# A block sum of a Winograd second layer, made by accumulating DMAs in place or by VectorE into a block of its own

## The chip, the cores and the metric

The kernel runs on one core of one Trainium2 chip. The metric is the device time of one execution in microseconds (us). TensorE (PE in the profile) does the matrix products, VectorE (DVE) and ScalarE (ACT) the elementwise work and the copies out of PSUM; GpSimd (POOL) here mostly issues DMAs, and SyncE (SP) issues the others. DMAs issued by POOL appear in the profile as queue q0 ("software_dynamic"), those of SP and ACT as q1 ("hardware_dynamic"); both are carried by the same 16 DMA engines.

## The reference

An attention with eight heads (three plain causal, five with a sink of 4 and a window of 64), whose output of 3072 tokens by 512 channels is the input of a mixture of four experts. Every token goes through all four:

```python
def _moe_ref(x, domain_probs, w1, w2):
    p = domain_probs / (domain_probs.sum(-1, keepdims=True) + 1e-09)
    out = np.zeros((N, D), dtype=np.float32)          # N 3072, D 512
    for e in range(E):                                # E 4
        h = np.maximum(x @ w1[e], 0.0)                # 512 -> 1024
        out += p[:, e:e + 1] * (h @ w2[e])            # 1024 -> 512
    return out.astype(np.float32)
```

## The kernel before

The tokens are cut into 24 tiles of 128. Tiles 0 to 3 go through both layers directly. The other 20 go two at a time, in ten **pairs** that are called here by their first tile: 4, 6, 8, ... 22. `pair_steps` makes one pair. Its inputs are scaled by the probabilities first (`scale_inputs`), so the second layer of all four experts is one product: hidden values of a pair (256 tokens, 4 x 1024 deep) by `w2` (4 x 1024 by 512).

That product is done with seven block products in place of eight (Strassen's scheme in Winograd's form). The hidden values lie in one SBUF tile `hA` (fp16) of five blocks, each 128 partitions by 16 x 128 elements. Four are the 2 x 2 blocks of the hidden values: A11 and A21 for the first half of each expert's hidden units (first and second token tile), A12 and A22 for the other half. Of the 16 columns of a block (`k`), four belong to each expert: 0 to 3 to expert 0, 4 to 7 to expert 1 and so on. The operand sums are

- S1 = A21 + A22 (`first_sum`),
- S2 = S1 - A11 (`second_sum`, in place of A11),
- S3 = A22 - S2 (`third_sum`),
- S4 = A12 - S2 (`fourth_sum`, in place of A12).

Before the change S1 has the fifth block and S3 takes the place of A21.

The order on TensorE within a pair: first layer 1, expert by expert; then the seven products, each of 16 matmuls with 256 columns (line 1387), in the order A11, A12, S2, S1, S3, S4, A22. Between their halves, steps of the attention of later tokens are put in until about pair 16. `second_sum(0)` makes the columns of experts 0 and 1 after the first product, `second_sum(1)` those of experts 2 and 3 in the middle of the second product. The third product is the first that reads S2.

Layer 1 has two forms. `plain_layer1(e)` yields four steps of eight matmuls (line 1207), each followed by a ReLU on ScalarE (line 1216) that writes two blocks for two columns. `winograd_layer1(e)` yields seven steps of eight small matmuls (line 1236); the last block that it writes is A21, by a ReLU on ScalarE at its end (line 1286). Which expert takes which form depends on the pair:

- pairs 4 to 16: experts 0, 1, 2 plain (twelve steps in that order), expert 3 by Winograd, mixed in;
- pair 18: experts 0 and 1 plain, 3 and 2 by Winograd;
- pair 20: experts 3 and 2 by Winograd, then expert 1 by Winograd mixed with expert 0 plain;
- pair 22, the last: all four by Winograd.

The order of the instructions on each engine is the order in which the program emits them (a manual schedule); `order` in `pair_steps` is a list of steps with an operation to emit after each group of steps. Every engine takes its own instructions strictly in turn. Waits are put in by dependency: an instruction waits until the last writer or reader of what it touches is done. A wait of a DMA is taken by the engine that issues it, before it issues.

POOL's queue also holds the loads of the attention, in the program's order: for each step of the attention five loads of values into `vS` (line 306), each waiting for the matmuls that read the old values, then three loads of keys (`k_rows`) and three of queries (`q`, line 219) and three of `vR` (line 304).

Touched by the change: the names S1, S2, S3 (line 979), `first_sum` (line 1180), and the lists in `pair_steps`.

Of the kernel before, what the change touches and what calls it, by code (L numbers as in the profile page):

```python
# [14 lines left out]
ALU = mybir.AluOpType  # L15
# [4 lines left out]
def kernel(  # L20
# [77 lines left out]
    gp = nc.gpsimd  # L98
# [9 lines left out]
    HT = F // P // 2  # L108
# [5 lines left out]
    EW = (E - 1, E - 2)  # L114
# [291 lines left out]
    for h in range(H):  # L406
        if h == 2:
            nc.sync.dma_start(
                out=v_s32, in_=v[0, :, 0:NS, :].rearrange("h r d -> r h d")
# [16 lines left out]
        out=probs,  # L426
        in_=moe_domain_probs[0 : NPL * P, :].rearrange("(t p) e -> p t e", p=P),
    )
    nc.sync.dma_start(
        out=p_in.rearrange("t x e -> t (x e)"),  # L430
        in_=moe_domain_probs.rearrange("(t x) e -> t (x e)", x=P),
# [543 lines left out]

    hA16 = hA
    blocks = hA.rearrange("p (b k x) -> p b k x", b=5, k=KT)
    A11, A21, A12, A22, S1 = (blocks[:, n, :, :] for n in range(5))
    S2, S3, S4 = A11, A21, A12

    def whole_b(k, n, e, ft):
        return w2sb[:, e * FTP + k * HT + ft, n * HN : (n + 1) * HN]
# [25 lines left out]
    def first_weight_sums(e):  # L1008

        return [  # L1010
            lambda: minus(t1[e, 0], w1_part(e, 0, 1), w1_part(e, 0, 0)),
            lambda: minus(t1[e, 1], w1_part(e, 1, 1), t1[e, 0]),
            lambda: minus(t1[e, 2], w1_part(e, 1, 0), t1[e, 1]),
            lambda: minus(w1_part(e, 0, 1), w1_part(e, 1, 1), w1_part(e, 0, 1)),
        ]
# [11 lines left out]
    EW3 = E - 3  # L1027
# [22 lines left out]
    def last_weight_sum(e):  # L1050

        minus(b_rows(0, 1, e), b_rows(1, 1, e), b_rows(0, 1, e))
# [79 lines left out]
    def load_probs(nt0):  # L1132
        pB_of[nt0] = moe.tile([P, PT, E, P], FP32, name="pB", tag="pB", bufs=1)
        rows = p_rows[nt0 : nt0 + PT, :]
        nc.sync.dma_start(
            out=pB_of[nt0].rearrange("p t e x -> p (t e x)"),
            in_=bass.AP(rows.tensor, rows.offset, [[0, P], [1, PT * E * P]]),
        )
# [8 lines left out]
    def scale_inputs(nt0, e):  # L1147

        if xs_of[0] is None:
            xs_of[0] = moe.tile([P, XS], FP16, name="xs", tag="xs", bufs=1)  # L1150
        xs = scaled(e)
        for g, c0, t0, n in pieces(nt0):
            require(g)
            xin = xT[g][:, :, c0 : c0 + n * P].rearrange("p c (t x) -> p c t x", t=n)
            o = xs[:, :, t0 * P : (t0 + n) * P].rearrange("p c (t x) -> p c t x", t=n)
            pb = pB_of[nt0][:, t0 : t0 + n, e, :]
            pb = pb.rearrange("p t (c x) -> p c t x", c=1)
            nc.vector.tensor_tensor(  # L1158
                out=o, in0=xin, in1=pb.to_broadcast([P, DMP, n, P]), op=ALU.mult
            )  # L1160
# [11 lines left out]
    def scaled_sums(e):  # L1172

        nc.vector.tensor_tensor(
            out=x_sum(e, 0), in0=x_part(e, 1, 0), in1=x_part(e, 1, 1), op=ALU.add
        )
        minus(x_sum(e, 1), x_sum(e, 0), x_part(e, 0, 0))
        minus(x_part(e, 1, 0), x_part(e, 0, 0), x_part(e, 1, 0))

    def first_sum(e, n=1):  # L1180
        k = slice(e * HT, (e + n) * HT)
        nc.vector.tensor_tensor(
            out=S1[:, k, :], in0=A21[:, k, :], in1=A22[:, k, :], op=ALU.add
        )
# [8 lines left out]
    def two(nt0):  # L1193
        return nt0 >= pairs[-LAST]

    def three(nt0):
        return nt0 >= pairs[-2]

    def pair_steps(nt0, nxt):

        def plain_layer1(e):
            xs = scaled(e)
            for f0 in range(0, FTP, 2):
                ps = bank()
                for f in range(2):
                    for ct in range(DMP):
                        nc.tensor.matmul(  # L1207
                            out=ps[:, f * PC : (f + 1) * PC],
                            lhsT=w1_tile(e, ct, f0 + f),
                            rhs=xs[:, ct, :],  # L1210
                            start=(ct == 0),
                            stop=(ct == DMP - 1),
                        )
                b0 = 2 * (f0 // HT)
                k0 = e * HT + f0 % HT
                nc.scalar.activation(  # L1216
                    out=blocks[:, b0 : b0 + 2, k0 : k0 + 2, :].rearrange(
                        "p t f x -> p f t x"
                    ),
                    in_=ps.rearrange("p (f t x) -> p f t x", f=2, t=2),  # L1220
                    func=AF.Relu,
                )
                yield 2 * DMP * mm_ns(PC), 0.5
# [69 lines left out]
        a, b = (winograd_layer1(e, *y) for e, y in zip(EW, (banks, banks[::-1])))  # L1293
        if three(nt0):
# [5 lines left out]
            b = winograd_layer1(EW[1], *more_banks, more_kept)  # L1300
            third = winograd_layer1(EW3, *banks)
            if nxt is None:
                second_set.add(0)
                fourth = winograd_layer1(0, *more_banks, more_kept)

        more, last_more = [], None
        if nt0 == pairs[-LAST - 2]:
            room_for_more_sums()
            more = first_weight_sums(EW[1])
        elif nt0 == pairs[-LAST - 1]:  # L1310
            last_more = first_weight_sums(EW[1])[3]
        elif nt0 == pairs[-3]:
            room_for_third()
            more = first_weight_sums(EW3)
            last_more = more[3]
        elif nt0 == pairs[-2]:
            room_for_fourth()
            more = first_weight_sums(0)
            last_more = more[3]
        if not two(nt0):  # L1320
            n = itertools.chain(*(plain_layer1(e) for e in range(E - 1)))
            order = (
                ((n,), lambda: scale_inputs(nt0, 1)),
                ((n,), more[0] if more else None),
                ((n, a), lambda: last_weight_sum(E - 1) if nt0 == pair0 else None),
                ((n, a), None),
                ((n, a), lambda: scale_inputs(nt0, 2)),
                ((n, a), lambda: load_probs(nxt)),
                ((n, a), more[1] if more else None),
                ((n, a), more[2] if more else None),  # L1330
                ((n, a), lambda: first_sum(0, 2)),
                ((n,), None),
                ((n, n), lambda: first_sum(2, 2)),
                ((), lambda: scale_inputs(nxt, 1) if two(nxt) else None),
            )
        elif nxt is None:
            order = (
                ((), lambda: scaled_sums(EW[1])),
                ((a, b, a, b), None),
                ((a, b, a, b), lambda: scaled_sums(EW3)),  # L1340
                ((a, b, a, b, a, b), lambda: scaled_sums(0)),
                ((third, fourth, third, fourth), lambda: first_sum(EW[0])),
                ((third, fourth, third, fourth), lambda: first_sum(EW[1])),
                ((third, fourth, third, fourth), None),
                ((third, fourth), lambda: (first_sum(EW3), first_sum(0))),
            )
        elif three(nt0):
            n = plain_layer1(0)
            order = (
                ((), lambda: scaled_sums(EW[1])),  # L1350
                ((a, b, a, b), lambda: load_probs(nxt)),
                ((a, b, a, b), None),
                ((a, b, a, b), None),
                ((a, b), lambda: scaled_sums(EW3)),
                ((n,), more[0]),
                ((third, third, n), lambda: first_sum(EW[0])),
                ((third, third, n), more[1]),
                ((third, third, n), lambda: (first_sum(EW[1]), first_sum(0))),
                ((third,), lambda: (first_sum(EW3), more[2]())),
            )  # L1360
        else:
            n = itertools.chain(plain_layer1(0), plain_layer1(1))
            order = (
                ((a, a, n), more[0] if more else None),
                ((a, a, n), lambda: load_probs(nxt) if nxt else None),
                ((a, a, n), more[1] if more else None),
                ((n,), lambda: scaled_sums(EW[1])),
                ((a, b, n), more[2] if more else None),
                ((b, b, n), lambda: first_sum(0)),
                ((b, b, n), lambda: first_sum(EW[0])),  # L1370
                ((b, n, b), lambda: (first_sum(1), first_sum(EW[1]))),
            )
        for steps, op in order:
            for x in steps:
# [98 lines left out]
        if last:  # L1473

            r = slice((nt0 + 1) * P, (nt0 + 2) * P)
            for c in (slice(0, HN // 2), slice(HN // 2, HN)):
                z = bank()[:, c]
                for k in range(KT):
                    nc.tensor.matmul(  # L1479
                        out=z,  # L1480
# [6 lines left out]
                    out=o[:, 1, c], in0=z, in1=s[:, 3, c], op=ALU.add  # L1487
# [158 lines left out]
```

## Time and profile before

| | |
|---|---|
| median of 3 runs | 376.64 us (376.29 to 377.06) |
| span of the profiled execution | 374.9 us |
| granted TensorE clock | 1.000 |
| PE busy | 367.2 us (98%) |
| VectorE busy | 284.3 us (76%), 610 instructions |
| ScalarE busy | 227.2 us (61%) |
| POOL busy | 113.1 us (30%), 155 instructions |
| q0, packets' time as a share of 16 engines' span | 58.8% |

The profiled execution's span runs from its first to its last instruction; its own time beside the unprofiled runs isn't given, and the median of those is 1.7 us above the span. The pairs take the span from about 88 us to its end. Their third products start at 107.59 (pair 4), 139.19, 168.18, 197.48, 226.98 (pair 12), 255.60, 286.88, 312.69, 337.79 (pair 20) and 363.12 us (pair 22), as the timeline of TensorE has them. In the rows of a timeline the first column is the start in us from the span's start, the second the duration in us; "x3" means that three instructions in a row are merged, and the brackets at the end say how long the engine had been idle and for what.

### The profile page before, as it was taken

The page shows a single profiled execution, that of the slowest core. Times are in us where ns is not written, and L with a number is a line of the kernel's source. Part 1 is how long each engine was busy: PE and PEld are TensorE (multiplying, and loading weights), DVE is VectorE, ACT ScalarE, POOL GpSimd, SP SyncE. Part 2 cuts the span into 40 slices and gives each one's busy share as a digit, 9 for nine tenths or more (in the row PEclk, how much of TensorE's full clock was granted, in tenths as well). Part 3 has the DMA queues.
Part 4 walks back from the last instruction along what each step waited for, and adds up shares of the span by engine and source line. Part 5 has one row for each costly group of instructions (what it writes and reads, how often), then busy time and mean ns, then how long its engine had stood idle before and what let it go on. Part 6 is the DMA issues. An engine that isn't in the chain of part 4 may idle for free.

```text
span 374.9 us, 10290 instructions
## 1 busy us (share of the span) xinstructions
PE 367.2 (98%) x4200; PEld 310.5 (83%) x4200; DVE 284.3 (76%) x610; ACT 227.2 (61%) x475; POOL 113.1 (30%) x155
## 2 busy tenths in 40 slices
PE   8899999999999999999999999999999999999996
PEld 4755466668998988999989898998899998998996
DVE  7775768697788669868658858957767868989882
ACT  3863478547785785765676955784777361450630
POOL 8924573872057038115601650320000000000000
PEclk9999999999999999999999999999999999999999
DMA  8999999999599599988904990951220300300101
GB/s 163 158 202 208 197 183 192 183 201 110 97 111 155 94 97 116 159 111 61 208 10 61 170 158 15 125 134 14 71 69 3 104 13 0 115 2 3 57 2 58
DMA packets 123748, 39.25 MB, mean 105 GB/s; under 512 B 113728, under 2 KB 116356, under 8 KB 123700
## 3 DMA queue, kind: packets, MB, share of 16 engines
q0 software_dynamic: 85824, 19.01, 58.8%
q1 hardware_dynamic: 36276, 19.18, 21.9%
q8 instruction: 33, 0.54, 0.6%
q10 hardware_dynamic: 1600, 0.39, 0.5%
q14 instruction: 15, 0.12, 0.1%
HBM read 44.89 MB, written 6.34 MB: 137 GB/s over the span
## 4 chain that ended last, share of the span: by engine, by line
PE 87%; DMA 7%; POOL 3%; DVE 1%; ACT 0%; issue 0%; POOLq 0%
PE pO L1387 31%; PE pA L1207 22%; PE pO L1236 9%; DMA w2sb<-in_moe_w_dram 7%; PE pO L1094 6%; PE pA L678 5%; PE pA L1073 5%; PE pV L1236 2%; PE pV L734 2%; PE pA L1236 2%; PE pV L806 2%; POOL vS L310 1%; POOL vR L304 1%; DVE xs L1158 1%; PE pA L1479 0%; POOL early L472 0%
## 5 line engine op out<-in xcount | busy, mean ns | idle before, releaser
L1387 PEld LDWEIGHTS <-hA 128*128 128x128 f16 x1104 | 104.9, 98 | 12.2
L1207 PE MATMUL pA<-xs,w1sb 128*128 128x256 f16 x768 | 97.2, 272 | 0.0
L1207 PEld LDWEIGHTS <-w1sb 128*128 128x128 f16 x768 | 71.8, 98 | 7.6
L1387 PE MATMUL pO<-w2sb,hA 128*128 128x256 f16 x640 | 76.7, 272 | 0.0
L696 ACT ACTIVATE es<-pA 128x384 f16<-128x384 f32 (+2 forms) x122 | 59.2, 512 | 27.1 <-PE pA L678 23.3
L1216 ACT ACTIVATE hA<-pA 128x512 f16<-128x512 f32 x96 | 57.2, 597 | 29.0 <-PE pA L1207 26.7
L306 POOL DMA_DIRECT2D vS<-in_v_dram x30 | 29.6, 986 | 111.9 <-PE pV L806 110.6
L1387 PE MATMUL pO<-tsb,hA 128*128 128x256 f16 x464 | 56.7, 272 | 0.0
L1158 DVE TENSOR_TENSOR xs<-xT,pB 128x1024 f16<-128x1024 f16 (+1 forms) x49 | 47.0, 978 | 1.4 <-DMA xT<-x_pair 1.4
L992 DVE TENSOR_TENSOR hA<-hA 128x1024 f16<-128x1024 f16 x60 | 39.5, 685 | 0.4
L1086 ACT ACTIVATE hA<-pA 128x384 f16<-128x384 f32 (+1 forms) x64 | 22.2, 385 | 19.4 <-PE pA L1073 18.7
L1236 PEld LDWEIGHTS <-w1sb 128*128 128x128 f16 x512 | 31.4, 98 | 1.4 <-issue 0.5
L1073 PE MATMUL pA<-xT,w1sb 128*128 128x384 f16 (+1 forms) x256 | 31.1, 273 | 0.7 <-DVE xT L829 0.3
L1094 PE MATMUL pO<-w2sb,hA 128*128 128x512 f16 x128 | 30.7, 379 | 0.3 <-DMA w2sb<-in_moe_w_dram 0.3
L1407 ACT COPY s<-pO 128x256 f32<-128x256 f32 x31 | 11.5, 372 | 27.7 <-PE pO L1387 21.9
L829 DVE TENSOR_TENSOR xT<-pV,rc 64x384 f16<-64x384 f32 x37 | 20.5, 555 | 10.3 <-ACT rc L834 7.9
L1073 PEld LDWEIGHTS <-w1sb 128*128 128x128 f16 x256 | 19.4, 98 | 9.7 <-issue 1.5
L824 ACT ACTIVATE rc<-pV,eps 64x384 f32<-64x384 f32 x37 | 21.3, 575 | 6.5 <-PE pV L806 5.9
L700 DVE TENSOR_TENSOR es<-es,mS 128x384 f16<-128x384 f16 (+1 forms) x40 | 13.7, 344 | 15.0 <-ACT es L696 15.0
L1246 ACT COPY s<-pO 128x512 f32<-128x512 f32 x39 | 22.7, 587 | 3.2 <-PE pO L1236 3.0
L1253 DVE CUSTOM_DVE_ANT_0 hA<-pO,s 128x512 f16<-128x512 f32 x26 | 17.7, 688 | 7.7 <-PE pO L1236 6.3
L678 PE MATMUL pA<-qT,kR 128*128 128x384 f16 (+2 forms) x120 | 22.9, 278 | 0.7 <-DVE kR L595 0.6
(170 smaller groups left out, 528.0 us busy)
## 6 DMA issues: line engine op xcount, KB each, us to landing
pB<-p_rows SPq DMA_DIRECT2D x10, 512.0 KB
out_dram<-o SPq DMA_DIRECT2D x19, 256.0 KB
w1sb<-in_moe_w_dram POOLq DMA_DIRECT2D x8, 512.0 KB, 9.2
w2sb<-in_moe_w_dram POOLq DMA_DIRECT2D x4, 1024.0 KB, 12.3
vS<-in_v_dram POOLq DMA_DIRECT2D x30, 112.0 KB, 4.3
k_rows<-in_k_dram POOLq DMA_DIRECT2D x18, 128.0 KB, 5.2
q<-in_q_dram POOLq DMA_DIRECT2D x18, 128.0 KB, 6.4
vR<-in_v_dram POOLq DMA_DIRECT2D x24, 48.0 KB, 5.8
```

The lines of the kernel that those rows point to most:

```text
L306: gp.dma_start(out=t[:, :, own_v(h)], in_=windows_of(v, b, h, c))
L678: nc.tensor.matmul(out=ps[:, o : o + nq], lhsT=key_tile(b, c, h, t), rhs=qTs[b, c][:, hp, q0 : q0 + nq], start=(n == 0 or not first), stop ...
L696: nc.scalar.activation(out=es[:, 0:cols], in_=ps[:, 0:cols], func=AF.Exp, scale=SC)
L992: nc.vector.tensor_tensor(out=out, in0=a, in1=b, op=ALU.subtract)
L1073: nc.tensor.matmul(out=pss[ft][:, 0:cols_n], lhsT=w1_tile(e, ct, ft), rhs=x[:, ct, :], start=(n == 0), stop=(n == DMP - 1),)
L1094: nc.tensor.matmul(out=ps_o, lhsT=hs[:, ft, j * P : (j + 1) * P], rhs=w2sb[:, e * FTP + ft, :], start=(ft == 0), stop=(ft == FTP - 1),)
L1158: nc.vector.tensor_tensor(out=o, in0=xin, in1=pb.to_broadcast([P, DMP, n, P]), op=ALU.mult)
L1207: nc.tensor.matmul(out=ps[:, f * PC : (f + 1) * PC], lhsT=w1_tile(e, ct, f0 + f), rhs=xs[:, ct, :], start=(ct == 0), stop=(ct == DMP - 1),)
L1216: nc.scalar.activation(out=blocks[:, b0 : b0 + 2, k0 : k0 + 2, :].rearrange("p t f x -> p f t x"), in_=ps.rearrange("p (f t x) -> p f t x" ...
L1236: nc.tensor.matmul(out=ps[:, f * P : (f + 1) * P], lhsT=w_tile(e, w[:, ct, :], f), rhs=a[:, ct, :], start=(first and f == 0 and ct == 0), ...
L1246: nc.scalar.copy(out=kept[n], in_=ps)
L1387: nc.tensor.matmul(out=ps, lhsT=a[:, k, :], rhs=b(k), start=(first and k == 0), stop=(k == KT - 1), skip_group_check=not first,)
```

## The change

`first_sum` becomes a DMA on POOL's queue that adds A22 onto A21 where A21 lies, so S1 takes the place of A21, and S3 gets the fifth block. VectorE's form remains under the name `last_first_sum`, now also in place, for the experts that a pair's layer 1 ends with. Pairs 4 to 16 each have one DMA for experts 0 and 1 (256 KB: 128 rows of 2 KB) and one for expert 3 (128 KB: 128 rows of 1 KB), with expert 2 left to VectorE; pair 18 has DMAs for experts 0 and 3, with 1 and 2 in one VectorE instruction; pair 20 DMAs for 3, 2 and 0, with 1 on VectorE; pair 22 DMAs for 3 and 2, with 0 and 1 in one VectorE instruction. In all 21 DMAs; VectorE's instructions of this kind go from 26 (14 of 128x1024, 12 of 128x512) to 10 (2 of 128x1024, 8 of 128x512).

```diff
-    A11, A21, A12, A22, S1 = (blocks[:, n, :, :] for n in range(5))
-    S2, S3, S4 = A11, A21, A12
+    A11, A21, A12, A22, S3 = (blocks[:, n, :, :] for n in range(5))
+    S1, S2, S4 = A21, A11, A12
...
     def first_sum(e, n=1):
+
+        k = slice(e * HT, (e + n) * HT)
+        gp.dma_start(out=S1[:, k, :], in_=A22[:, k, :], accum_op=ALU.add)
+
+    def last_first_sum(e, n=1):
         k = slice(e * HT, (e + n) * HT)
         nc.vector.tensor_tensor(
             out=S1[:, k, :], in0=A21[:, k, :], in1=A22[:, k, :], op=ALU.add
...
                 ((n, a), lambda: first_sum(0, 2)),
-                ((n,), None),
-                ((n, n), lambda: first_sum(2, 2)),
+                ((n,), lambda: first_sum(EW[0])),
+                ((n, n), lambda: last_first_sum(EW[1])),
...
                 ((third, fourth, third, fourth), lambda: first_sum(EW[0])),
                 ((third, fourth, third, fourth), lambda: first_sum(EW[1])),
                 ((third, fourth, third, fourth), None),
-                ((third, fourth), lambda: (first_sum(EW3), first_sum(0))),
+                ((third, fourth), lambda: last_first_sum(0, 2)),
...
                 ((third, third, n), lambda: first_sum(EW[0])),
                 ((third, third, n), more[1]),
                 ((third, third, n), lambda: (first_sum(EW[1]), first_sum(0))),
-                ((third,), lambda: (first_sum(EW3), more[2]())),
+                ((third,), lambda: (last_first_sum(EW3), more[2]())),
...
                 ((b, b, n), lambda: first_sum(0)),
                 ((b, b, n), lambda: first_sum(EW[0])),
-                ((b, n, b), lambda: (first_sum(1), first_sum(EW[1]))),
+                ((b, n, b), lambda: last_first_sum(1, 2)),
```

The four lists are those of pairs 4 to 16, of pair 22, of pair 20 and of pair 18. `EW[0]` is expert 3, `EW[1]` expert 2, `EW3` expert 1.

On POOL's queue the two DMAs of a pair stand, in pairs 4 to 12, behind the `vR` loads of the attention step before and ahead of the next `vS` loads; those of pair 14 stand behind the third of the last five `vS` loads and ahead of the other two; those of pairs 16 to 22 have nothing behind them. The orders on TensorE, ScalarE and SP stay as they were.

## The prediction, made before the changed kernel ran

> **What bounds it now.** First the chain of work that ended last (page), then the busy time of each engine over pairs 4 to 20. Columns of the second row: stretch, its length, then busy us (instructions) of PE, PEld, DVE, ACT, POOL, then clock, DMA share and GB/s.
>
> ```profile
> PE 87%; DMA 7%; POOL 3%; DVE 1%; ACT 0%; issue 0%; POOLq 0%
> 88.00:347.00 259.00, 258.87 (x3152) 235.57 (x3150) 200.10 (x425) 165.07 (x324) 54.81 (x61) 1.00 0.69 84
> ```
>
> TensorE sets the end, and from 88 to 347 us it is idle for 0.13 us in all. VectorE is busy for 200.10 of 259. So relief of VectorE can return next to nothing there, and anything that makes a third product wait is paid in full. Third, the removed work itself:
>
> ```profile
> L1182 DVE TENSOR_TENSOR hA<-hA x26: 415/677/693, 101.1 to 360.5; 128x1024 f16<-128x1024 f16 x14, 128x512 f16<-128x512 f16 x12
> who waited for it (us, times):
> ```
>
> Nothing is listed as having waited for it.
>
> **What it removes.** Twelve sums of 128x1024 by 0.685 us and four of 128x512 by 0.415 us: 8.2 + 1.7 = 9.9 us of VectorE. TensorE hides all of it, so I put the gain at 0.1 us, bounds 0 and 0.4 (the 0.13 us above, and some 0.3 us of like waits in pair 22's layer 1). S1 in A21's place costs nothing: the next pair's layer 1 overwrites A21 after the seventh product, and S1 was last read in the fourth. S3 in the fifth block costs nothing: its reader in the pair before is done more than 15 us earlier.
>
> **What it adds: a delay between the ReLU and S1.** VectorE started a sum 0.03 us after a ReLU (104.00 to 104.03). A DMA first has to be issued, moved and reported. The trace has no adding DMA. Nearest is a `vS` load that met an idle queue at 251.70, 112 KB; its window gives (packets, MB, share of 16 engines over 3.4 us; then KB and us to landing):
>
> ```profile
> q0 software_dynamic: 912, 0.11, 52.8%
> vS<-in_v_dram POOLq DMA_DIRECT2D x1, 112.0 KB, 3.4
> ```
>
> Of its 3.4 us, 0.98 is POOL's own and 1.8 packet time on each engine (52.8% of 3.4), whose packets overlap a little and lie within 1.4 us. A 128 KB sum has few long rows: 8 rows of 1 KB an engine, about 0.4 us (the output stores of 346 to 350 us: 288 packets, 34.8% of 16 x 4 us, 77 ns for 2 KB). **Low end**: 3.4 - 0.35 (POOL at 0.63, as for the `w1sb` loads) - 1.4 + 0.4, about 2.0 us. **High end**: the adding cuts rows into 128-byte pieces at the `vS` packets' 32 ns and reads twice: 128 pieces an engine, 4.1 us in place of 1.8: 5.7 us. I take 3.0 us, nearer the load, its nearest row, with a little off for long rows. For 256 KB add 0.4 to 4.1 us; I take 0.5.
>
> The Trainium skill ("Collectives: The Full Stack", The bandwidth ceiling: the fold count and why AG ≠ RS ≠ AR) speaks against the change: a DMA that adds reads two sources on one ring, and ran at half the rate of a copy. Its "DMA: Bandwidth & Descriptors" (Anatomy of one DMA — SWDGE (gpsimd) path) gives 2.0 us plus bytes at 436 GB/s, so an estimate by both pages is 2.6 us for 128 KB, against 3.4 us measured here for 112 KB in small rows; the sum below would fall by 0.4 us with it. No adding DMA is in this trace to decide it.
>
> **When it is due.** S2's first half must be written when the third product starts. The subtraction takes 0.69 us (128x1024, line 992) and I allow 0.1 us for two wake-ups, so S1 of experts 0 and 1 is due 0.79 us before the third product, that of experts 2 and 3 0.79 us before its middle. From the end of the ReLUs (lines 1216, 1286) this leaves 6.4 to 8.8 us for the first DMA and 5.5 to 7.6 us for the second in pairs 4 to 10, 14, 16; the tightest is pair 14 (248.35 to 254.81, 250.15 to 255.69). `second_sum` ran in these pairs 4.7 us or more after the ReLU, so with 3.0 to 3.5 us even VectorE's queue doesn't notice. Pair 18 leaves 9 us; pair 22 has its DMAs done 4 us ahead. Cost 0; the cover is gone above some 5 us.
>
> **Pair 20** is different: the DMA of expert 0 follows the last ReLU of plain layer 1, which is nearly the end of layer 1.
>
> ```profile
> 334.05 0.60 ACT L1216 ACTIVATE hA<-pA 128x512 f16<-128x512 f32 x1 [1.17 <-PE pA L1207]
> 334.29 3.66 PE L1387 MATMUL pO<-w2sb,hA 128*128 128x256 f16 x32
> 336.11 1.29 DVE L992 TENSOR_TENSOR hA<-hA 128x1024 f16<-128x1024 f16 x2
> 337.79 2.46 PE L1387 MATMUL pO<-tsb,hA 128*128 128x256 f16 x21
> ```
>
> The ReLU ends at 334.65, the third product starts at 337.79: S1 is due at 337.00. POOL wakes some 0.05 us after the ReLU (0.30 us after a matmul's modelled end, 103.54 to 103.84, against ScalarE's 0.25, 336.04 to 336.29). 334.70 + 3.0 = 337.70: **0.7 us** late, bounds 0 (2.0 us) and 3.4 (5.7 us). Behind the waiting `second_sum` on VectorE stand the other `second_sum` and the output sum of line 1410, whose PSUM bank the fourth product needs 1.75 us later: no further cost. Nothing else is on TensorE there to fill the gap.
>
> **Pair 12** meets loads in its queue. POOL is still issuing the `vR` loads when expert 1's ReLU ends (219.36), and q0 is full:
>
> ```profile
> 218.61 2.33 POOL L304 DMA_DIRECT2D vR<-in_v_dram  x3
> 218.76 0.60 ACT L1216 ACTIVATE hA<-pA 128x512 f16<-128x512 f32 x1 [0.72 <-PE pA L1207]
> 224.38 1.29 DVE L992 TENSOR_TENSOR hA<-hA 128x1024 f16<-128x1024 f16 x2
> ...
> vR<-in_v_dram POOLq DMA_DIRECT2D x1, 48.0 KB, 5.6
> ...
> 225.00:225.50 0.50, 0.50 (x7) 0.44 (x6) 0.50 (x2) 0.31 (x1) 0.00 (x0) 1.00 0.44 53
> 225.50:226.00 0.50, 0.50 (x7) 0.41 (x5) 0.17 (x1) 0.02 (x1) 0.00 (x0) 1.00 0.00 0
> ...
> 226.98 1.04 PE L1387 MATMUL pO<-tsb,hA 128*128 128x256 f16 x8
> ```
>
> The DMA can be issued at 220.94, but the last `vR` load, issued at 220.14, lands 5.6 us later at 225.76, its packets ending near 225.4 (DMA share 0.44, then 0.00). If the queue is served in order, the 256 KB follow: 0.65 us at 77 ns for 2 KB, 1.3 if read twice, 8.2 in doubled 128-byte pieces; I take 1.1. Plus 0.35 us to report: 226.85, due at 226.19: **0.65 us** late, bounds 0.2 and 7.8. Here `second_sum` holds VectorE 2.5 us past its old time, and masks (line 700), key copies (line 290) and later operand sums stand behind it; VectorE had 0.94 us of idle time to catch up and TensorE is 0.65 late itself, so some of it reaches a later product: **0.2 us**, bounds 0 and 1.
>
> **Moved past on the queues.** POOL's `vS` loads come more than 2 us after each pair's DMAs, except in pair 14, where the fourth (245.82) now stands behind DMAs that wait until 250.15, 5 us later; it is used by the last attention step near its end, and the fifth (251.70) moves by under 1 us: 0. SP has no new instruction; its transposes share the DMA engines with 384 KB more a pair, off the path.
>
> **Sum**: 0.7 + 0.65 + 0.2 - 0.1 = 1.45 us. The profiled span of 374.9 becomes 376.4; the runs' median stands 1.7 us above the span, so 376.64 becomes **378.1 us**.
>
> **Rivals.**
> *All hidden*: a small sum costs 2.2 us and its data run at the stores' rate. Pair 20 is then on time, pair 12 0.2 us late: 376.64 + 0.2 = 376.8 us. For it: long rows, SBUF to SBUF. Against: pair 20's 2.3 us, which the nearest row misses by 1.1.
> *The addition is slow* and most pairs pay: with 128-byte pieces read once (2.05 us of packets for 128 KB, 4.1 for 256 KB), the first DMA lands after 5.7 us, the second after 7.8, one alone after 3.65. Pair 14 is then 0.5 late, pair 12 4.5 (3.7 by its first DMA), pair 20 1.35, and VectorE's queue waits in every pair, some 1 us in all: 376.64 + 7.35 = 384.0 us. For it: no adding DMA was measured. Against: rows of 2 KB have no reason to be cut.
> *VectorE's relief shows* (faster): 9.9 us fewer on its queue bring masks and copies forward, and PE's short waits go, 0.13 us in the pairs to 20 and 0.3 in pair 22's layer 1: 376.2 us. It decides only if both late DMAs land within 2.3 us and behind no load. Against: to gain over 0.75 us there is no idle time to take.
> *It doesn't do what it says* is out: the DMAs stand on POOL's queue in program order.
>
> **How the numbers follow.** Forecast (two pairs late, own range 377.3 to 380) 0.53; all hidden 0.32; slow addition 0.11; relief 0.04, most of it for more than the rows let me see. 0.2%, 0.75 us, is about what a measurement of this kernel can tell from no change. A little of the forecast and of the relief lies within that, the slow case all beyond: faster 0.03, same 0.34, slower 0.63. The range goes from the relief's 376.2 to 381.6, where pair 12's first DMA pays 3.7 and pair 20 1.35 for once-read pieces, less 0.1; beyond lies most of the slow case.
>
> **What would show it.** Gaps of TensorE before the third product in pairs 12 and 20 alone; DMAs to `hA` landing after about 3 us, after 5 to 6 in pair 12; VectorE idle before line 992 (now 997) for a DMA there. Wrong, if these gaps are missing, if other pairs show them, or if PE's matmuls themselves slow down under the added traffic.

## The result, and the profile after

The changed kernel took a median of 379.69 us (four runs, 379.15 to 380.40) against 376.85 us of the kernel before (four runs, 376.29 to 377.65): a ratio of 1.0079, 95% interval 1.0066 to 1.0091, or 2.84 us more. The profiled execution's span is 378.1 us against 374.9.

The page of the changed kernel first: the busy time of each engine, and the chain of work that ended last, by engine.

```profile
PE 368.3 (97%) x4200; PEld 311.3 (82%) x4200; DVE 275.4 (73%) x594; ACT 227.2 (60%) x475; POOL 130.9 (35%) x176
...
PE 65%; issue 15%; DMA 10%; POOL 7%; DVE 2%; ACT 1%; POOLq 0%; SPq 0%; DVEq 0%
```

VectorE is busy for 8.9 us less (284.3 before; the prediction counted 9.9 taken off). TensorE has fallen from 87% of the chain to 65%. The chain in order of time (start, length, what) shows what has come in:

```profile
221.28 6.81 DMA hA<-hA
...
331.22 1.17 POOL hA L1183
...
337.30 2.63 DMA hA<-hA
```

It ends with two waits for adding DMAs and is followed back from each along POOL's queue, so long stretches of POOL's issuing and of its waiting ("issue") count as chain that are none: a share of the chain is not a loss. What TensorE waits for tells where the time went. The waits of TensorE come first, then one row of VectorE's; each row gives who waited, for whom, and us in total, times, the longest.

```profile
PE pO L1392 <- DVE hA L992: 1.9, 2, 1.4
...
PE pV L734 <- DVE es L700: 0.4, 1, 0.4
```

```profile
DVE hA L992 <- DMA hA<-hA: 5.1, 2, 3.6
```

Line 1392 holds the matmuls of the seven products (1387 before). Twice they waited for `second_sum` (line 992), and twice `second_sum` waited for an adding DMA. The timeline of the changed kernel puts the first of these in pair 12 (start, duration, engine, line; in brackets the idle time before and its releaser):

```profile
219.01 2.30 POOL L304 DMA_DIRECT2D vR<-in_v_dram  x3
221.28 0.96 POOL L1183 DMA_DIRECT2D hA<-hA  x1
223.66 0.86 POOL L1183 DMA_DIRECT2D hA<-hA  x1 [1.42 <-DMA v_sinks<-vS]
...
228.18 1.38 DVE L992 TENSOR_TENSOR hA<-hA 128x1024 f16<-128x1024 f16 x2 [3.57 <-DMA hA<-hA]
...
228.93 1.05 PE L1392 MATMUL pO<-tsb,hA 128*128 128x256 f16 x8 [1.37 <-DVE hA L992]
...
235.15 0.23 PE L734 MATMUL pV<-vR,es 128*128 128x65 f16 x2 [0.39 <-DVE es L700]
```

and the second in pair 20:

```profile
336.41 0.60 ACT L1221 ACTIVATE hA<-pA 128x512 f16<-128x512 f32 x1 [1.17 <-PE pA L1212]
...
337.30 0.84 POOL L1183 DMA_DIRECT2D hA<-hA  x1 [4.91 <-ACT hA L1221]
...
340.05 1.29 DVE L992 TENSOR_TENSOR hA<-hA 128x1024 f16<-128x1024 f16 x2 [1.50 <-DMA hA<-hA]
...
340.80 0.94 PE L1392 MATMUL pO<-tsb,hA 128*128 128x256 f16 x7 [0.49 <-DVE hA L992]
```

The idle time in a bracket is less than the delay, since the records of the matmuls overlap. The delay itself is read by setting the same matmul of both traces side by side. Each column gives by how much a version's matmul starts later than before's beyond what had already gathered; the first column is the lag at the third product of pair 4, the others are the steps up to the third product named, and the last goes on to the last matmul.

| | up to pair 4 | to 10 | to 12 | to 14 | to 18 | to 20 | to the end | from pair 10 on |
|---|---|---|---|---|---|---|---|---|
| after | +0.42 | 0.00 | **+1.53** | **+0.58** | -0.16 | **+0.65** | +0.18 | +2.78 |

The first 0.42 us arise around the first loads (by 20 us of the span; the first adding DMA is issued at 99.60), and up to pair 4 every profiled execution differs, from -0.24 to +1.18 in the runs below. They are no part of the change. From pair 10 on the sum is 2.78 us, against 2.84 by the medians. The 1.53 are pair 12's third product, the 0.58 an attention matmul that stands among its later products (line 734, at 235.15), the 0.65 pair 20's third product. In pairs 4 to 10, 14 and 16 nothing moved. The 0.18 arise in pair 22; of the runs below only e7 has them too, though most have that pair's DMAs, and no run tells the cause.

In the list of DMA issues (output and input, queue, count, KB each, median us to landing) the adding DMAs of the whole span are

```profile
hA<-hA POOLq DMA_DIRECT2D x7, 256.0 KB, 3.7
hA<-hA POOLq DMA_DIRECT2D x14, 128.0 KB, 3.0
```

On an idle queue 128 KB took 2.63 to 2.69 us and 256 KB 3.30 to 3.35; beside the attention's loads, in pairs 4 to 8, 3.7 to 5.1, and nobody waited there, as the spare 5.5 to 8.8 us of the prediction let one expect.

### The profile page after: what moved, and what is told of

It is laid out like the page before. It is cut to its first block, busy times and chain, and to the rows that moved or that the text cites. A ratio compares the mean times of both kernels' runs of the same rounds, so it can differ in the third digit from the quotient of the medians.

```text
span 378.1 us, 10320 instructions
## 1 busy us (share of the span) xinstructions
PE 368.3 (97%) x4200; PEld 311.3 (82%) x4200; DVE 275.4 (73%) x594; ACT 227.2 (60%) x475; POOL 130.9 (35%) x176
## 4 chain that ended last, share of the span: by engine, by line
PE 65%; issue 15%; DMA 10%; POOL 7%; DVE 2%; ACT 1%; POOLq 0%; SPq 0%; DVEq 0%
PE pO L1392 21%; PE pA L1212 17%; DMA w2sb<-in_moe_w_dram 7%; PE pO L1094 6%; PE pO L1241 6%; PE pA L1073 5%; PE pA L678 4%; DMA hA<-hA 2%; PE pV L734 2%; PE pV L806 1%; PE pV L1241 1%; PE pA L1241 1%; POOL vR L304 1%; POOL vS L306 1%; POOL vS L310 1%
## 5 line engine op out<-in xcount | busy, mean ns | idle before, releaser
L1183 POOL DMA_DIRECT2D hA<-hA x21 | 18.4, 921 | 146.6 <-ACT hA L1221 87.7
L306 POOL DMA_DIRECT2D vS<-in_v_dram x30 | 29.7, 1000 | 53.4 <-PE pV L806 51.4
```

The costliest lines, as they stand in the source:

```text
L306: gp.dma_start(out=t[:, :, own_v(h)], in_=windows_of(v, b, h, c))
```

## The experiments

All nine start from the changed kernel. Ratios are to the kernel before, measured beside it; the steps are read as in the table above.

| | median us | ratio (95%) | to 12 | to 14 | to 18 | to 20 | to the end |
|---|---|---|---|---|---|---|---|
| after | 379.69 | 1.0079 (1.0066 to 1.0091) | +1.53 | +0.58 | -0.16 | +0.65 | +0.18 |
| e1, pair 12 by VectorE | 377.32 | 1.0015 (1.0006 to 1.0024) | 0.00 | 0.00 | -0.16 | +0.70 | -0.01 |
| e2, pair 20's last by VectorE | 379.21 | 1.0073 (1.0054 to 1.0091) | +2.08 | +0.57 | -0.16 | 0.00 | -0.02 |
| e3, both | 376.69 | 1.0000 (0.9992 to 1.0009) | 0.00 | 0.00 | -0.16 | 0.00 | -0.02 |
| e4, all by VectorE, in place | 376.75 | 1.0001 (0.9992 to 1.0009) | 0.00 | 0.00 | -0.16 | 0.00 | -0.02 |
| e5, pair 12's loads behind | 377.77 | 1.0039 (1.0013 to 1.0066) | 0.00 | +0.47 | -0.16 | +0.65 | -0.01 |
| e6, no sums | 377.30 | 1.0018 (1.0010 to 1.0027) | 0.00 | 0.00 | -0.16 | 0.00 | -0.02 |
| e7, copies that don't add | 378.76 | 1.0047 (1.0032 to 1.0063) | +1.47 | +0.49 | -0.16 | 0.00 | +0.18 |
| e8, all DMAs brought in time | 378.00 | 1.0034 (1.0021 to 1.0046) | 0.00 | +0.47 | -0.16 | +0.92 | -0.02 |
| e9, one small DMA in pair 12 | 377.55 | 1.0020 (1.0008 to 1.0032) | 0.00 | +0.94 | -0.16 | 0.00 | -0.02 |

**e1, e2, e3: one place at a time.** The two pairs where a wait showed get VectorE's form back, alone and together.

```diff
 # e1 and e3: pair 12
-                ((n, a), lambda: first_sum(0, 2)),
-                ((n,), lambda: first_sum(EW[0])),
+                ((n, a), lambda: (last_first_sum if nt0 == 12 else first_sum)(0, 2)),
+                ((n,), lambda: (last_first_sum if nt0 == 12 else first_sum)(EW[0])),
...
 # e2 and e3: pair 20
-                ((third, third, n), lambda: (first_sum(EW[1]), first_sum(0))),
+                ((third, third, n), lambda: (first_sum(EW[1]), last_first_sum(0))),
```

> In pair 12 alone the sums go back to VectorE; all other DMAs stay. Theory 'two places' (only pair 12's DMAs behind the loads and pair 20's DMA of expert 0 cost time): the 1.5 us before pair 12's third product and the 0.6 us of VectorE's arrears behind it go, so this is 2.1 us under the changed kernel, some 0.7 us over the kernel before (377.5 us). Rival 'spread' (21 DMAs slow all pairs a little, as more traffic or more work on GpSimd): one pair of nine gives back 0.3 us or less. Rival 'start' (the 0.4 us that the two profiles differ by in their first 6 us belongs to the change): 0.4 us more than the first theory says, 1.1 us over the kernel before.

> In pair 20 alone the sum of expert 0 goes back to VectorE, as a sum of its own ahead of expert 1's. 'Two places': the 0.65 us before pair 20's third product go, pair 12's 2.1 us stay: 2.2 us over the kernel before (378.9 us). In its profile no idle time of TensorE before the third product of pair 20, and the same 1.4 us before that of pair 12. 'Spread': no change to speak of (0.1 us). If pair 12's delay is mostly chance of one execution (its loads landed 0.5 us later than in the profile before), pair 12's wait differs here by some tenths.

> Both edits together; 18 DMAs stay. 'Two places': the time of the kernel before within 0.2 us, for 18 of 21 DMAs are free and taking 7 us of work off VectorE brings nothing. 'Spread': 2 us over the kernel before. 'Relief counts' (VectorE's shorter queue is worth something once no DMA is late): 0.4 us or more under the kernel before. 'Start': 0.4 us over it.

TensorE's waits that bear on it, of e1:

```profile
PE pO L1392 <- DVE hA L992: 0.5, 1, 0.5
```

and of e2:

```profile
PE pO L1392 <- DVE hA L992: 1.9, 1, 1.9
...
PE pV L734 <- DVE es L700: 0.4, 1, 0.4
```

Each takes away exactly its own wait, and e1 the later wait of line 734 as well, so that one follows from pair 12. With both on VectorE nothing is left: 376.69 us, although 18 of the 21 DMAs are still there. So the whole loss lies in three DMAs, two in pair 12 and one in pair 20; the other 18 cost nothing and earn nothing.

**e4 and e6: what the relief of VectorE is worth.** e4 keeps the exchanged blocks, with all sums by VectorE; e6 has no sums at all.

```diff
 # e4, in first_sum
-        gp.dma_start(out=S1[:, k, :], in_=A22[:, k, :], accum_op=ALU.add)
+        nc.vector.tensor_tensor(
+            out=S1[:, k, :], in0=A21[:, k, :], in1=A22[:, k, :], op=ALU.add
+        )
...
 # e6, in first_sum and last_first_sum
+        return
```

> All sums on VectorE, each at its place in the program's order of the changed kernel, but S1 still in A21's place and S3 in the fifth block: the exchange of the blocks alone. 'Two places': same as the kernel before within 0.2 us. If the exchange itself costs (a longer wait of a ReLU or of the third sum on the block's last reader), it shows here as the part of the 2.8 us that no DMA is to blame for.

> No sum S1 at all, by VectorE or DMA: A21 stands in its place, so this part of the computation is left out. It bounds what any relief of VectorE from these sums can bring. Theory: TensorE has no idle time that these sums cause, so the same as the kernel before within 0.2 us (376.5 us). Rival 'relief counts': 0.4 us or more under the kernel before, which a change that costs nothing elsewhere could have won.

e4 ties with before, so the exchange of blocks costs nothing. In all columns e6's matmuls move as e4's, to 0.01 us: with VectorE freed of every one of these sums, no matmul comes earlier than with all of them on it. The relief is worth nothing, not even the 0.1 us that I gave it. (The -0.16 us in pair 18 stand in every version, e4 too, where VectorE does it all, so they are no relief either; their cause no run tells.) e6's time is nevertheless 0.18% (0.7 us) over before's. Its trace has that behind the last matmul, 3.84 us to the end of the span in place of 3.09 to 3.15 in the others: an output store lands later. One 8 KB packet of queue q14, which the profile calls "instruction", stands among these stores in e6 (372.80 to 373.11) and comes well before the last matmul in all other versions (351 to 363). That it is the cause no run isolates.

**e5: the loads ahead of pair 12's DMA, or the DMA itself?** The nine loads of the last attention step (keys, queries and `vR`), which stand ahead of pair 12's DMAs in POOL's queue, go behind them.

```diff
+    deferred = []
...
-                ((n,), lambda: first_sum(EW[0])),
+                ((n,), lambda: (first_sum(EW[0]), deferred and loads(deferred.pop()))),
...
-            if 1 < a < G - 1:
+            if a == G - 2:
+                deferred.append(a + 1)
+            elif 1 < a < G - 1:
```

> The changed kernel, but the last nine loads of keys, queries and values of the attention stand behind pair 12's two DMAs on GpSimd's queue, not ahead of them. Theory 'place in the queue': pair 12's first DMA then meets a queue without loads, lands some 3.3 us after its issue like those of pairs 10, 14 and 16, and the 1.5 to 2.1 us before pair 12's third product go, with the 0.56 us behind them; pair 20's 0.65 us stays: 377.3 us. Rival 'traffic': the DMA engines are busy with the 512 KB load of probabilities and the output stores at that time, the place doesn't matter, and 1 us or more stays. Third possibility: the loads, some 9 us later, now hold back the transposes of keys (SP) and the last attention step, and a wait of TensorE appears between pairs 14 and 16.

POOL's timeline in e5, then the DMA issue of the first row (us to landing last):

```profile
220.00 0.90 POOL L1184 DMA_DIRECT2D hA<-hA  x1 [6.28 <-ACT hA L1222]
221.80 0.86 POOL L1184 DMA_DIRECT2D hA<-hA  x1 [0.90 <-ACT hA L1292]
222.42 2.94 POOL L219 DMA_DIRECT2D k_rows<-in_k_dram  x3
225.08 2.92 POOL L219 DMA_DIRECT2D q<-in_q_dram  x3
227.67 2.85 POOL L304 DMA_DIRECT2D vR<-in_v_dram  x3
```

```profile
hA<-hA POOLq DMA_DIRECT2D x1, 256.0 KB, 3.5
```

In the changed kernel the same DMA took

```profile
hA<-hA POOLq DMA_DIRECT2D x1, 256.0 KB, 6.8
...
vR<-in_v_dram POOLq DMA_DIRECT2D x1, 48.0 KB, 6.2
```

Its place behind the loads cost it 3.3 us: 3.5 after issue ahead of them, 6.8 behind them, and the wait before pair 12's third product is gone. That settles the place. It did not win the whole of pair 12 back: 0.47 us are lost later, at a matmul of line 734 that waits for a mask. Two things could have set VectorE's queue back there: it waited 0.47 us for the second DMA (225.61), and two key copies (lines 290 and 294) ran longer while POOL was issuing the loads that now come later. Set beside e3, whose TensorE stands within 0.02 us of e5's at that time, VectorE's rows tell the two apart. In e5:

```profile
226.95 0.29 DVE L700 TENSOR_TENSOR es<-es,mC 128x256 f16<-128x256 f16 x1 [0.65 <-ACT es L696]
...
227.98 0.86 DVE L290 COPY kS<-kT 64x1736 f16<-64x1736 f16 x1
228.76 0.41 DVE L294 COPY kS<-kT 64x56 f16<-64x56 f16 x1
229.20 0.29 DVE L700 TENSOR_TENSOR es<-es,mC 128x256 f16<-128x256 f16 x1
```

and in e3:

```profile
226.97 0.29 DVE L700 TENSOR_TENSOR es<-es,mC 128x256 f16<-128x256 f16 x1 [1.03 <-ACT es L696]
...
228.00 0.61 DVE L290 COPY kS<-kT 64x1736 f16<-64x1736 f16 x1
228.53 0.17 DVE L294 COPY kS<-kT 64x56 f16<-64x56 f16 x1
228.73 0.29 DVE L700 TENSOR_TENSOR es<-es,mC 128x256 f16<-128x256 f16 x1
```

The wait for the DMA is made up by 226.95, out of VectorE's idle time. Behind the two copies e5 is 0.47 us late, so the loss comes from them.

**e7: is it the adding?** The same DMAs as plain copies, without the addition.

```diff
-        gp.dma_start(out=S1[:, k, :], in_=A22[:, k, :], accum_op=ALU.add)
+        gp.dma_start(out=S1[:, k, :], in_=A22[:, k, :])
```

> The same 21 DMAs without the addition (A22 copied over A21; the sum of these experts is left out), to price the adding itself. If an adding row costs twice a plain one because its destination is read too, 2 KB rows take about 80 to 95 ns in place of 185, 128 KB land after 2.2 us in place of 2.63, 256 KB after 2.6 in place of 3.3; pair 20's wait falls from 0.65 to 0.2 us, pair 12's from 1.5 to 0.8 or so, and the whole to 1.5 us over the kernel before. If the fixed part is all that counts, landings and time stay those of the changed kernel (2.8 us over).

Pair 20's small DMA in two windows of equal content, first the changed kernel's (1.7 us long), then e7's (1.2 us long): queue, packets, MB, share of 16 DMA engines.

```profile
q0 software_dynamic: 144, 0.13, 53.4%
```

```profile
q0 software_dynamic: 48, 0.13, 30.6%
```

The adding form moved its 128 KB in 128 packets of 1 KB (and 16 small ones): 53.4% of 16 x 1.7 us is 14.5 us of packet time, 113 ns for each KB. The plain copy had 32 packets of 4 KB and 30.6% of 16 x 1.2, 5.9 us or 46 ns for each KB. So adding costs about 2.5 times the packet time. To landing:

```profile
hA<-hA POOLq DMA_DIRECT2D x1, 128.0 KB, 1.9
```

against 2.6 with the addition, of which 0.3 is POOL's own issuing (0.54 us in place of 0.84). That difference of 0.7 us is pair 20's whole delay: its step is 0.00 here. In pair 12 the step is nearly as large as with the addition (+1.47): the copy landed 6.7 us after its issue, 1.39 us after the last `vR` load, as in the changed kernel (228.09 and 226.70, also 1.39). So in pair 20 the adding is what makes the DMA late. For pair 12 this run alone doesn't say that the adding is free: its profile is of the slowest of four runs (379.54; the fastest took 377.96), and another packet ended later there than in the changed kernel, as told under pair 12 below.

**e8: can all DMAs be brought in time?** e5's edit, and pair 20's expert 0 finished a step earlier in layer 1.

```diff
-                ((third, third, n), more[1]),
-                ((third, third, n), lambda: (first_sum(EW[1]), first_sum(0))),
+                ((third, n, n, third), more[1]),
+                ((third, third), lambda: (first_sum(EW[1]), first_sum(0))),
```

> All 21 DMAs, with both causes taken away by order alone: pair 12's DMAs ahead of the loads, and in pair 20 the last step of expert 0's plain layer 1 put 3 steps of expert 1's (some 1.3 us) earlier, so that expert 0's DMA starts as much earlier against the third product. Theory: no wait before either third product, the time of the kernel before within 0.2 us (376.7 us): a change that costs nothing and wins nothing. If VectorE's relief is worth something, 0.4 us or more under it. If pair 20's wait isn't the ReLU-to-DMA-to-sum chain, 0.65 us stays.

A miss. No third product waits, but the new order of layer 1 costs pair 20 0.92 us, more than the wait that it avoids. A wait of TensorE in e8 that the others don't have:

```profile
PE pO L1242 <- ACT s L1252: 0.3, 1, 0.3
```

The last four of `winograd_layer1`'s steps now stand together, where at most two did, and the sixth waits for ScalarE's copy of the PSUM bank that the fourth filled. These four start at 332.80, 333.25, 334.13 and 334.86, the first product at 335.52: where an unhindered step takes 0.45 us, the last three lose 0.43, 0.28 and 0.21, in sum the 0.92. The trace names the copy for 0.27 of it and nothing for the rest. The order before hid it.

**e9: less data behind the loads.** Pair 20 by VectorE; in pair 12 only expert 3's DMA (128 KB) stays.

```diff
-                ((n, a), lambda: first_sum(0, 2)),
+                ((n, a), lambda: (last_first_sum if nt0 == 12 else first_sum)(0, 2)),
...
-                ((third, third, n), lambda: (first_sum(EW[1]), first_sum(0))),
+                ((third, third, n), lambda: (first_sum(EW[1]), last_first_sum(0))),
```

> Pair 20 as in the run with its sum on VectorE, and in pair 12 only the smaller DMA (expert 3, 128 KB) stays; experts 0 and 1 go to VectorE. It splits pair 12's cost. The smaller DMA stands behind the same loads and lands at about 228 us, so VectorE is held nearly as long, but what waits is the second half of S2, which the third product needs only at its middle (228.2 us). Theory: no wait before the third product, some 0.5 us at its middle, and the 0.5 us of VectorE's arrears further on stay: 0.8 to 1.1 us over the kernel before. If the arrears came from the third product's delay and not from VectorE being held, 0.5 us or less. If the size of the first DMA (256 KB) had made pair 12 late, nothing is late here: the time of the kernel before.

VectorE and TensorE in e9's timeline:

```profile
227.35 0.69 DVE L992 TENSOR_TENSOR hA<-hA 128x1024 f16<-128x1024 f16 x1 [2.48 <-PE pA L678]
```

```profile
227.06 1.04 PE L1392 MATMUL pO<-tsb,hA 128*128 128x256 f16 x8
...
228.26 1.04 PE L1392 MATMUL pO<-tsb,hA 128*128 128x256 f16 x8
...
233.63 0.24 PE L734 MATMUL pV<-vR,es 128*128 128x65 f16 x2 [0.76 <-DVE es L700]
```

The row of VectorE names TensorE as what ended 2.48 us of idle time, but the DMA landed at 227.23, 0.12 us before the start, the step from landing to VectorE that pair 20 shows too (339.92 to 340.05): a wait for several semaphores carries one name. Neither the third product nor its middle (228.26) waits. Yet TensorE loses 0.94 us, 6.6 us later, at a mask that stood behind the waiting `second_sum`. This is the clearest row of the study: a wait on VectorE alone, with no late product, costs as much as the forecast of pair 12 as a whole (0.85).

No version beat the kernel before. e3 and e4 tie with it.

## Why the prediction came out as it did

The forecast was 378.1 us with 376.2 to 381.6; the mechanism (two pairs late, the rest hidden) and both places were right, and the size was about half.

| step of the sum | predicted | measured |
|---|---|---|
| pair 20, DMA late | 0.7 (0 to 3.4) | 0.65; 0.70 in e1 |
| pair 12, first DMA late | 0.65 (0.2 to 7.8) | 1.53; 2.08 in e2, 1.47 in e7 |
| pair 12, VectorE's arrears | 0.2 (0 to 1) | 0.58; 0.94 alone in e9 |
| other pairs | 0 | 0.00 in 4 to 10, 14 and 16; -0.16 in 18 and +0.18 in 22 |
| relief | -0.1 (0 to -0.4) | none (e6 beside e4) |
| sum | 1.45 | 2.78 |

*Pair 20* was right with two errors that cancel. POOL started 0.29 us after the ReLU's end (337.01 to 337.30), not 0.05; the DMA landed after 2.63 us, not 3.0. The sums are 2.92 and 3.05. The estimate that the prediction worked out from the Trainium skill for 128 KB ("Collectives: The Full Stack", The bandwidth ceiling: the fold count and why AG ≠ RS ≠ AR, with "DMA: Bandwidth & Descriptors", Anatomy of one DMA — SWDGE (gpsimd) path) was 2.6 us and so the better one; for 256 KB the same sum is an estimate of 3.2 us, with 3.3 measured. Its rule that an adding DMA moves at half the rate of a copy also agrees in kind, with 113 against 46 ns for each KB in the windows above.

*Pair 12* is the step that failed, by its size. Of the 1.53 us, 0.65 was forecast. The first DMA landed at 228.09; the forecast 226.85, moved by the 0.42 us of the start-up, is 227.27. Of these 0.82 us, 0.52 is that the last `vR` load itself landed later (226.70, against 225.76 + 0.42), and 0.30 that the DMA followed it by 1.39 us and not by the forecast 1.09 (226.85 less 225.76). I had taken the backlog's end from one execution as if it were fixed: from the last `vR` issue to its landing before shows 5.63 us, e6 5.68, e1 and e3 6.00 and 6.01 and e4 7.28, all with no DMA behind it in pair 12, and after 6.18. So the 0.52 lies within what executions without that DMA differ by.

What the prediction had at nothing is a packet of 16 KB on queue q8, which the profile calls "instruction". Before, it stood at 225.23 to 226.18, where the prediction read the DMA share as 0.00. A single packet, it presumably keeps a single one of the 16 DMA engines, and rows that wait behind it there come last. In e4, which has no adding DMA, q0 has no packet from 226.97 to 227.55, and the last four of the loads go as the q8 packet ends (227.57). Its row before (a window of 1.0 us), in e4 (1.1 us) and in the changed kernel (1.6 us):

```profile
q8 instruction: 1, 0.02, 6.0%
```

```profile
q8 instruction: 1, 0.02, 5.5%
```

```profile
q8 instruction: 1, 0.02, 5.6%
```

By their shares of 16 engines that is 0.96, 0.97 and 1.43 us. In the changed kernel it ends at 226.31. One engine's part, with the 128 rows spread evenly, is eight rows, 0.19 us each there, in sum 1.5 us: 227.8, and the last row ended at 227.75. In e2 it is 226.18 + 1.5, and the last row ended at 227.62; against TensorE's lag the packet ends 0.53 us later than in the changed kernel, and the delay is 0.55 larger. The same sum fits within 0.1 us for the 128 KB DMA of e9 and the second DMA of e5, which had no loads ahead and still took 3.69 us where its like in pairs 14 and 16 took 2.65 and 2.66. With before's packet the forecast would have been 226.18 + 1.5 + 0.35 = 228.03, an estimate of 1.8 us late, between the 1.53 and the 2.08.

So the adding, the doubt that the range was built on, does count in pair 12. In e7 the packet ended 0.65 us later than in the changed kernel (227.47 and 226.31, less the lags of 0.93 and 0.42), while four packets of 4 KB at 0.18 us take 0.7 us in place of 1.5 (227.47 + 0.7 + 0.35 = 228.52, and it landed at 228.54). By these rows the adding makes an estimated 0.8 us of the delay, which e7's later packet hid. The packets' times fit, but the trace doesn't name the engine of a packet and no run moved this one: the account is read from the traces, not shown by an edit.

*The arrears* were put at 0.2 us by setting a 2.5 us hold of VectorE against 0.94 us of its idle time and TensorE's own lateness. The hold was longer (3.57 us idle), but even e9's 2.48 us cost 0.94 us of TensorE where TensorE wasn't late itself. In the changed kernel TensorE's lateness of 1.53 us hides part of it, and 0.58 is left. The reasoning was right in kind; the price lay near the upper bound, because in pair 12 VectorE's queue carries the masks and key copies of attention and has hardly a gap.

*The relief* rests on TensorE's 0.13 us of idle time over pairs 4 to 20 and fell out as read: nothing. Of the rivals, the slow addition is out (no pair but the two waited; 3.3 us for 256 KB, not 5.7), all hidden is out by e1 and e2, and the relief by e6.

## What to carry to other kernels

Work taken off an engine that doesn't end the chain is worth what the bounding engine's idle time holds, here 0.13 us; the price of the way that replaces it is paid wherever that way is late, so look for the tightest pair and not for the average one (18 of 21 DMAs were free, three cost 2.8 us). A DMA that stands in a queue behind loads lands with the last of its rows (in pair 12 they ran from 224.16 to 227.75), here 6.8 us after issue and not 3.5. A backlog's end read from one trace needs a margin (the same load landed 5.63 to 7.28 us after its issue in these runs), and a single packet on another queue belongs in it. Where an engine waits for a DMA in program order, price what stands behind the wait on that engine too: in e9 that was all of the loss.

## What the runs showed of the hardware that was not expected

- VectorE's fp16 copies can run longer beside POOL's DMA issue. Of one shape in the kernel before, the first while POOL issued the `vR` loads (117.61 to 119.94), the second with POOL idle:

```profile
118.05 0.82 DVE L290 COPY kS<-kT 64x1736 f16<-64x1736 f16 x1
...
124.33 0.61 DVE L290 COPY kS<-kT 64x1736 f16<-64x1736 f16 x1
```

  and 0.86 in e5, where it cost TensorE 0.47 us. It isn't so each time: the first copy in the changed kernel, also beside the issue of the `vR` loads (117.83 to 120.22), took

```profile
118.60 0.61 DVE L290 COPY kS<-kT 64x1736 f16<-64x1736 f16 x1
```

  The Trainium skill ("SBUF — State Buffer", Who interferes with whom) says that a copy in a 2-port mode and GpSimd exclude each other from a shared port, the later one blocked for the other's whole instruction. The longer rows agree that the two can meet, though with some 0.2 us lost and not the whole of a DMA's issue (0.8 to 0.9 us). That these copies run in such a mode no run shows, nor what decides when they meet.
- POOL itself is slow to start after ScalarE, 0.29 us, and before its second DMA in pair 12 it was idle for 1.42 us. The timeline above names a DMA of `v_sinks` for that; by the trace's semaphores it was the third `k_rows` load, whose semaphore this DMA uses too. That load landed at 223.08, 222.30 and 222.34 in the changed kernel, e2 and e7, and the DMA was issued 0.58 us later each time; in e5, with the loads behind it, it was issued 0.29 us after its ReLU.
- The plain copy's rows were joined to packets of 4 KB, the adding form's stayed at one row each (1 or 2 KB).
